# Moving transposes from TensorE to the DMA engines in a gated linear attention followed by a GELU layer, on one Trainium2 core

## The chip, the cores and the metric

The kernel runs on one core of one Trainium2 chip. The metric is the device time of one launch in microseconds (us), the median over runs. A profile of one execution gives what each engine did; its span runs from the first to the last instruction, and the execution's own time is a little longer than that span.

## The reference

```python
def _attn_ref(q, k, v, f_logit):                 # (4, 8, 768, 48) each
    f = 1.0 / (1.0 + np.exp(-f_logit))
    for t in range(S):
        state = f[:, :, t, :, None] * state + np.einsum('bhd,bhe->bhde', k[:, :, t], v[:, :, t])
        y[:, :, t] = np.einsum('bhd,bhde->bhe', q[:, :, t], state)
    return y

def _moe_ref(x, w_in, w_out):                    # (3072, 384), (384, 2048), (2048, 384)
    h = x @ w_in
    g = 0.5 * h * (1.0 + erf(h / sqrt(2)))
    return g @ w_out

def reference(**kwargs):
    attn_out = _attn_ref(q, k, v, f_logit)
    x = attn_out.transpose(0, 2, 1, 3).reshape(B * S, H * D)
    return _moe_ref(x, w_in, w_out)              # (3072, 384) float32
```

A recurrence over 768 steps with a decay per channel (4 batches, 8 heads, 48 channels) makes 3072 rows of 384 numbers. Each row then passes through a layer of 2048 hidden values with the exact GELU.

## The kernel before, in words

The 3072 rows are cut into 24 chunks of 128 rows; two chunks make a unit, so that there are 12 units, numbered from 0, and 6 chunks to a batch. Units 0, 1 and 2 are loaded in another layout ("pair"), with two neighbouring rows in one partition.

For each unit `decays` computes on ScalarE Exp (E) and Ln (L) of the logits; on TensorE the sums of the logs over the rows of a chunk (C, by products with triangular matrices); on ScalarE the exponentials of these sums, RG (to scale keys), GT (to scale queries) and GL (decay over a whole chunk); on VectorE the scaled keys KP and queries QP, in bf16; on GpSimd the cast of the values, VC.

`turn` transposes KP and QP. For each chunk TensorE makes four transposes of each (Tk, Tq: matmuls of 128x128 against an identity) into one PSUM bank, and VectorE copies the bank into the buffer `kq` (KQ). `attn_nat` (and `attn_pair` for pair units) then makes the scores (A, which reads `kq`), VectorE masks them (AM), TensorE updates the state (S; `carry` decays it on VectorE and GpSimd: R, T, SB) and multiplies scores and state with the values (Y, or YI and YX in pair units). `outputs` casts Y to bf16 on VectorE (YB), transposes it on TensorE (XT, three 128x128 matmuls) and copies it to the buffer `xT` on VectorE (X).

`ffn_group` takes the two chunks of a unit as a group of 256 rows. F1 is 8 operations of 6 matmuls of 128x256, each followed by one GELU on ScalarE (GE). F2 is, for each chunk, 4 operations of 4 matmuls of 128x384; the result leaves PSUM on ScalarE (O) and is stored (st). Exp and Ln share one ScalarE table and GELU needs another, so that each change between them costs a table load.

The order of the work on each engine is not written by hand. A planner (class `Plan`) knows for every operation an engine, an assumed duration, what it reads and writes, its buffers and a priority. It places operations greedily, those that can start first ahead of others, then by priority; what it makes is a fixed order of instructions on every engine. Engines then run this order and wait for each other through semaphores. The attention's operations have priority over those of the layer behind it. The planner treats DMAs as one more engine: `load` lists the loads in a fixed order (`LOADS`: units 0 and 1, the four blocks of `w_in`, unit 2, the four blocks of `w_out`, units 3 to 11), loads of inputs and stores of results are issued by SyncE's queue (SP), weights by GpSimd, and weights and inputs take turns by waiting for one another.

PSUM has 8 banks: four for F1 and F2 (`s_fh`), two for scores (`s_ap`), two for all else (`s_m`). There are 4 buffers for each of keys, queries and values, 3 for logits, 3 for `kq` and 4 for `xT`.

Of the kernel before, what the change touches and what calls it, by code (L numbers as in the profile page):

```python
# [16 lines left out]
TABLE = 1.28  # L17
# [40 lines left out]
class Op:  # L58
    __slots__ = ("eng", "dur", "fn", "bufs", "prio", "deps", "table", "start", "end", "vis", "seq", "name",
                 "left", "outs", "inst", "chain")  # L60


class Plan:
# [6 lines left out]
    def add(self, eng, dur, fn, rd=(), wr=(), bufs=(), prio=0.0, deps=(), table=None, name="", chain=None):  # L70
        o = Op()
        o.eng, o.dur, o.fn, o.bufs, o.prio, o.table, o.name = eng, dur, fn, tuple(bufs), prio, table, name
        o.start = o.end = o.vis = o.inst = None
        o.chain = chain
        o.seq = len(self.ops)
        d = list(deps) + ([chain] if chain else [])
        for k in rd:
            d += self.w.get(k, [])
        for k in wr:
            d += self.w.get(k, []) + self.r.get(k, [])  # L80
        for k in rd:
            self.r.setdefault(k, []).append(o)
        for k in wr:
            self.w[k] = [o]
            self.r[k] = []
        o.deps = list({id(x): x for x in d if x is not o}.values())
        for b in o.bufs:
            b.users.append(o)
        self.ops.append(o)
        return o  # L90

    def run(self):
        free = dict.fromkeys(list(LAT), 0.7)
        free["DMA"] = 1.8
        act = None
        for o in self.ops:
            o.outs = []
        for o in self.ops:
            o.left = len(o.deps)
            for d in o.deps:  # L100
                d.outs.append(o)
        ready = [o for o in self.ops if not o.left]
        placed = []
        while ready:
            best = None
            for o in ready:
                t = free[o.eng]
                for d in o.deps:
                    v = d.end if d.eng == o.eng and (o.eng != "DMA" or d is o.chain) else d.vis
                    t = v if v > t else t  # L110
                ok, taken = True, {}
                for b in o.bufs:
                    if b.slot is None:
                        v, k = b.slots.free(), taken.get(id(b.slots), 0)
                        if len(v) <= k:
                            ok = False
                            break
                        t = max(t, v[k][0])
                        taken[id(b.slots)] = k + 1
                if not ok:  # L120
                    continue
                x = t
                if o.table and act and o.table != act:
                    x = max(t, min(t + 2 * TABLE, max([d.vis for d in o.deps] + [0.0]) + PATIENCE))
                key = (int(x * 20 + 0.999), o.prio, o.seq)
                if best is None or key < best[0]:
                    best = (key, t, o)
            if best is None:
                raise RuntimeError("no operation can be placed: %s" % [o.name for o in ready[:20]])
            _, t, o = best  # L130
            d = o.dur
            if o.table and o.table != act:
                act = o.table
                d += TABLE
            o.start, o.end = t, t + d
            o.vis = o.end + LAT[o.eng]
            free[o.eng] = o.end
            for b in o.bufs:
                if b.slot is None:
                    b.slot = b.slots.free()[0][1]  # L140
                    b.slots.who[b.slot] = b
            ready.remove(o)
            placed.append(o)
            for n in o.outs:
                n.left -= 1
                if not n.left:
                    ready.append(n)
        if len(placed) != len(self.ops):
            raise RuntimeError("operations that wait for each other")
        placed.sort(key=lambda o: (o.start, o.seq))  # L150
        self.placed = placed
        return placed
# [4 lines left out]

SIZES = [2] * 12
PAIRS = [0, 1, 2]
LOADS = ["u0", "u1", "i0", "i1", "i2", "i3", "u2", "o0", "o1", "o2", "o3"]  # L160
# [4 lines left out]
def kernel(  # L165
# [172 lines left out]
    for what in LOADS:  # L338
        m = int(what[1:])
        if what[0] == "u":  # L340
            x = U[m]
            names = (("fl", f_logit), ("kt", k), ("qt", q), ("vt", v))
            if x["pair"]:
                for nm, a in names:
                    load("sp", lambda x=x, nm=nm, a=a, m=m: nc.sync.dma_start(  # L345
                        out=x[nm].t().rearrange("p (h x) -> p h x", h=H), in_=srcp(a, m)),
                        [(nm, 2 * m), (nm, 2 * m + 1)], [x[nm]], 1.2, f"{nm}{m}")
            else:
                for j in range(2):
                    for nm, a in names:  # L350
                        load("sp", lambda x=x, nm=nm, a=a, m=m, j=j: nc.sync.dma_start(
                            out=half(m, x[nm], j), in_=src(a, 2 * m + j)),
                            [(nm, 2 * m + j)], [x[nm]], 1.05, f"{nm}{m}.{j}")
        elif what[0] == "i":
            load("pool", lambda m=m: nc.gpsimd.dma_start(out=win[m], in_=win_src[:, :, 512 * m:512 * m + 512]),
                 [f"win{m}"], [], 2.2, what)
        else:
            load("pool", lambda m=m: nc.gpsimd.dma_start(out=wout[m], in_=wo_src[m]), [f"wout{m}"], [], 2.2, what)


    def decays(u):
# [6 lines left out]
        P.add("ACT", 0.72, lambda: nc.scalar.activation(fl.t(), fl.t(), AF.Exp, scale=-1.0),  # L368
# [5 lines left out]
        P.add("ACT", 0.72, lnop, rd=[("e", u)] + z_lf, wr=[("lf", u)], bufs=[fl, lf], table="exp", prio=pr, name=f"L{u}")  # L374
        gps = [s_m.new(), s_m.new()]
        for j, n in enumerate(ns):
# [5 lines left out]
            def cum(j=j, g=gps[j]):  # L382
# [9 lines left out]
                if j:  # L392
# [6 lines left out]
                  bufs=[lf, gps[j], gt, rg, y["kp"], y["qp"], gl], prio=pr, name=f"C{n}")  # L399
# [19 lines left out]
            P.add("POOL", 0.47, lambda y=y, j=j: nc.gpsimd.tensor_copy(  # L419
# [3 lines left out]
    St = {}  # L423

    def turn(u, kq):


        for j in range(2):
            n = 2 * u + j
            kp, qp = X[n]["kp"], X[n]["qp"]  # L430
            tp = s_m.new()
# [10 lines left out]
            def trans(i, sr, tpv=tpv):  # L442
                for p in range(P2):
                    nc.tensor.transpose(tpv()[:, i, p, :], sr.t()[:, 2 * p:2 * p + 2, :], ident)  # L444
            P.add("PE", 0.225, lambda kp=kp, trans=trans: trans(0, kp), rd=[("kp", n), "ident"], wr=[("tk", n)],
                  bufs=[tp, kp, kq], prio=pr + 4, name=f"Tk{n}")
            P.add("PE", 0.225, lambda qp=qp, trans=trans: trans(1, qp), rd=[("qp", n), "ident"], wr=[("tq", n)],
                  bufs=[tp, qp], prio=pr + 4, name=f"Tq{n}")
            P.add("DVE", 0.61, lambda tpv=tpv, kqv=kqv: nc.vector.tensor_copy(  # L449
# [11 lines left out]
    def carry(n, sp, mm, mmdur, mmrd, mmbufs, first_c):  # L461
# [4 lines left out]
        if mm is not None:  # L466
            P.add("PE", mmdur, mm, rd=mmrd, wr=[("sp", n)], bufs=[sp, tn] + mmbufs + ([] if first_c else [rr]),
                  prio=pr + 3.5, name=f"S{n}")
# [24 lines left out]
    def outputs(n, yp, pair):  # L493
# [3 lines left out]
        yb, xp = X[n]["yb"], s_m.new()  # L497
        P.add("DVE", 0.475, lambda: nc.vector.tensor_copy(yb.t(), yp.t()[:, 0:HD]),  # L498
              rd=[("yp", n)], wr=[("yb", n)], bufs=[yp, yb], prio=pr + 2, name=f"YB{n}")

# [6 lines left out]
        P.add("PE", 0.17, xmm, rd=[("yb", n), "ident"], wr=[("xp", n)], bufs=[yb, xp, xT], prio=pr + 1, name=f"XT{n}")  # L507

        def xcopy():
            to = xT.t()[:, :, j * C:(j + 1) * C]  # L510
            if pair:
                nc.vector.tensor_copy(to.rearrange("a i (p s) -> a i s p", s=2), xpv().rearrange("a i (s p) -> a i s p", s=2))
            else:
                nc.vector.tensor_copy(to, xpv())
        P.add("DVE", 0.27, xcopy, rd=[("xp", n)], wr=[("x", n)], bufs=[xp, xT], prio=pr + 1, name=f"X{n}")
# [6 lines left out]
    def attn_nat(u):  # L522
        kq = s_kq.new()
        turn(u, kq)
        for j in range(2):
# [11 lines left out]
            P.add("PE", 0.42, amm, rd=[("kq", n)], wr=[("ap", n)], bufs=[kq] + aps + ams, prio=pr + 3, name=f"A{n}")  # L537
# [13 lines left out]
            def ymm(j=j, ams=ams, vb=vb, yp=yp, osb=osb):  # L551
                if osb is not None:
                    inter(yp, lambda p: kq.t()[:, 1, p, j, :], osb, True)
                for hh in range(2):
# [5 lines left out]
            P.add("PE", 0.36 + (0.175 if c else 0), ymm,  # L560
                  rd=[("am", n, 0), ("am", n, 1), ("vb", n), ("kq", n)] + ([("sb", n - 1, 0), ("sb", n - 1, 1)] if c else []),
                  wr=[("yp", n)], bufs=[yp, x["yb"], vb, kq] + ams + ([osb] if c else []), prio=pr + 2, name=f"Y{n}")
            outputs(n, yp, False)

    def attn_pair(u):
# [8 lines left out]
        for jk in range(2):  # L574
            aps = [s_ap.new(), s_ap.new()]
            ams.append([s_am.new(), s_am.new()])

            def amm(jk=jk, aps=aps):
                for p in range(P2):
# [7 lines left out]
                  prio=pr + 3, name=f"A{u}.{jk}")  # L587
# [3 lines left out]
        def smm():  # L591
            for p in range(P2):
# [7 lines left out]
              wr=[("sp", n) for n in ns[:len(sps)]], bufs=sps + kps + vbs, prio=pr + 3.5, name=f"S{u}")  # L600
# [9 lines left out]
        def intra():  # L610
            for hh in range(2):
# [11 lines left out]
              prio=pr + 2, name=f"YI{u}")  # L623
        for cc, n in enumerate(ns):
# [3 lines left out]
            P.add("PE", 0.26, lambda cc=cc, o=o: inter(yps[cc], lambda p: kq.t()[:, 1, p, cc, :], o, False),  # L628
                  rd=[("yi", n), ("sb", n - 1, 0), ("sb", n - 1, 1)] + [("kq", m) for m in ns], wr=[("yp", n)],
                  bufs=[yps[cc], kq, o], prio=pr + 2 + 10 * cc, name=f"YX{n}")  # L630
        for cc, n in enumerate(ns):
            outputs(n, yps[cc], True)

    def ffn_group(g, gate):
# [10 lines left out]
        for u in range(FO // pk):  # L645
            hps = s_fh.new()

            def f1(u=u, hps=hps):
                for i in range(pk):
# [6 lines left out]
                  wr=[("h", g, u)], bufs=[xT, hps, gT], prio=pr, name=f"F1.{g}.{u}")  # L656
# [4 lines left out]
        for s_ in range(s):  # L661
# [11 lines left out]
            P.add("DMA", 0.55, lambda n=n, osb=osb: nc.sync.dma_start(out=out[n * C:(n + 1) * C, :], in_=osb.t()),  # L673
# [13 lines left out]
    state = {}  # L687
    for o in P.placed:
        if o.table and state.get("t") != o.table:
# [36 lines left out]
```

## Time and profile before

| | us |
|---|---|
| median of 3 runs (lowest to highest) | 203.27 (203.03 to 203.34) |
| the profiled execution's own time | 202.79 |
| its span | 200.9 |

| engine | busy us | share of the span | instructions |
|---|---|---|---|
| TensorE, matmuls (PE) | 182.2 | 91% | 2010 |
| TensorE, weight loads (PEld) | 141.7 | 71% | 2010 |
| VectorE (DVE) | 103.7 | 52% | 210 |
| ScalarE (ACT) | 143.4 | 71% | 243 |
| GpSimd (POOL) | 52.4 | 26% | 116 |

The time is 1.89 us above the span in the profiled execution, which itself is 0.48 us under the median. A line number such as L444 is a line of the kernel. "Landing" of a DMA is the time from its issue until its completion is seen. In a chain of waits each step is followed back to what released it; a share in it is a share of the way to the end, not of an engine's work. Shares of busy time are means over stages that differ: at the start the loads are awaited, in the middle the attention and the layer run together, and at the end only the layer is left.

### The profile page before, as it was taken

Reading aid. Unit: us, or ns where it says so; the run is one execution under the profiler, and the core shown is the slowest. Engines: PE = TensorE matmul, PEld = TensorE weight load, DVE = VectorE, ACT = ScalarE, POOL = GpSimd, SP = SyncE. Lnnn points to the kernel's source line nnn. Section 1 sums busy time; section 2 is a strip of 40 time slices with the busy share of each in tenths; the row PEclk is TensorE's granted clock in tenths of the full one; section 3 lists DMA queues with packets and bytes.
Section 4 is the critical chain, followed back from the end, with each engine's and each line's share of the span. In section 5 each row is a group of like instructions: output and inputs, shape, how many; then the busy total and the mean of one; then the engine's idle time right before and its main releaser. Section 6 shows DMA issues by size and latency. Waiting matters only on the chain.

```text
span 200.9 us, 4982 instructions
## 1 busy us (share of the span) xinstructions
PE 182.2 (91%) x2010; PEld 141.7 (71%) x2010; DVE 103.7 (52%) x210; ACT 143.4 (71%) x243; POOL 52.4 (26%) x116
## 2 busy tenths in 40 slices
PE   0677989999989997997999999999999999999992
PEld 0446667687678687666868958967877969696961
DVE  4479661274386685887559728759778400000000
ACT  3642069989899979986999999769565828273740
POOL 7369236041133434105145411115303000000000
PEclk9999999999999999999999999999999999999999
DMA  6999999999899989989999993011001011110102
GB/s 155 261 224 172 175 269 189 182 220 202 181 216 195 182 203 186 203 177 210 182 197 214 191 214 96 3 39 39 3 0 65 16 42 39 38 44 11 68 0 78
DMA packets 93013, 27.04 MB, mean 135 GB/s; under 512 B 87872, under 2 KB 92480, under 8 KB 92992
## 3 DMA queue, kind: packets, MB, share of 16 engines
q1 hardware_dynamic: 90816, 23.60, 53.7%
q0 software_dynamic: 2176, 3.15, 9.4%
q8 instruction: 15, 0.25, 0.5%
q14 instruction: 6, 0.05, 0.1%
HBM read 25.17 MB, written 4.72 MB: 149 GB/s over the span
## 4 chain that ended last, share of the span: by engine, by line
PE 57%; ACT 20%; DMA 13%; SPq 3%; issue 3%; DVE 2%; POOL 1%; ACTq 0%; DVEq 0%
PE ps L667 25%; PE ps L652 20%; ACT L692 8%; ACT gT L657 6%; DMA fl<-in_f_logit_dram 5%; DMA win<-in_moe_w_in_dram 4%; DMA kt<-in_k_dram 3%; PE ps L444 3%; SPq L345 2%; ACT fl L368 2%; PE ps L535 2%; ACT lf L373 2%; PE ps L506 1%; ACT rg L400 1%; PE ps L385 1%
## 5 line engine op out<-in xcount | busy, mean ns | idle before, releaser
L652 PE MATMUL ps<-xT,win 128*128 128x256 bf16 x576 | 72.7, 277 | 3.1 <-ACT gT L657 3.0
L667 PE MATMUL ps<-wout,gT 128*128 128x384 bf16 x384 | 70.1, 326 | 0.4 <-DMA wout<-in_moe_w_out_dram 0.2
L652 PEld LDWEIGHTS <-win 128*128 128x128 bf16 x576 | 61.4, 115 | 6.0 <-issue 3.5
L657 ACT ACTIVATE gT<-ps 128x512 bf16<-128x512 f32 x96 | 53.1, 602 | 7.9 <-PE ps L652 5.6
L667 PEld LDWEIGHTS <-gT 128*128 128x128 bf16 x384 | 35.1, 97 | 21.3 <-ACT gT L657 1.3
L692 ACT ACT_TABLE_LOAD x29 | 37.2, 1283 | 0.5
L413 DVE TENSOR_TENSOR kp<-kt,rg 128x384 bf16<-128x384 f32 x24 | 13.9, 579 | 24.1 <-ACT rg L400 24.0
L671 ACT ACTIVATE osb<-ps 128x384 f32<-128x384 f32 x24 | 11.8, 493 | 20.2 <-PE ps L667 20.0
L456 DVE TENSOR_TENSOR am<-ps,mask 128x512 bf16<-128x512 f32 x36 | 23.1, 684 | 5.9 <-PE ps L535 5.8
L419 POOL CAST vb<-vt 128x384 bf16<-128x384 f32 x24 | 13.1, 554 | 43.7 <-DMA vt<-in_v_dram 43.4
L482 POOL TENSOR_TENSOR tn<-rr,gl 128x384 f32<-128x384 f32 x16 | 13.6, 850 | 41.5 <-DVE rr L480 38.7
L368 ACT ACTIVATE fl<-fl 128x768 f32<-128x768 f32 x12 | 10.3, 859 | 18.0 <-DMA fl<-in_f_logit_dram 17.9
L498 DVE CAST yb<-ps 128x384 bf16<-128x384 f32 x24 | 13.0, 553 | 11.9 <-PE ps L557 9.0
L449 DVE COPY kq<-ps 128x1024 bf16<-128x1024 bf16 x24 | 16.4, 685 | 3.3 <-PE ps L444 3.1
L487 POOL CAST sb<-tn 48x192 bf16<-48x192 f32 x40 | 15.3, 383 | 8.4 <-DVE tn L476 6.5
L400 ACT ACTIVATE rg<-ps 128x384 f32<-128x384 f32 x24 | 11.9, 495 | 6.8 <-PE ps L387 3.5
L416 DVE TENSOR_TENSOR qp<-qt,gt 128x384 bf16<-128x384 f32 x24 | 14.4, 601 | 0.2 <-ACT gt L402 0.2
L402 ACT ACTIVATE gt<-ps 128x384 f32<-128x384 f32 x24 | 11.9, 496 | 0.0
L444 PE MATMUL ps<-ident,kp 128*128 128x128 bf16 x96 | 10.2, 234 | 0.3 <-DVE kp L413 0.3
L456 DVE TENSOR_TENSOR am<-ps,maskp 128x512 bf16<-128x512 f32 x12 | 7.7, 685 | 5.4 <-PE ps L583 5.4
L444 PE MATMUL ps<-ident,qp 128*128 128x128 bf16 x96 | 10.2, 234 | 0.3 <-DVE qp L416 0.3
L373 ACT ACTIVATE lf<-fl 128x768 bf16<-128x768 f32 x12 | 10.1, 843 | 0.3
(58 smaller groups left out, 150.6 us busy)
## 6 DMA issues: line engine op xcount, KB each, us to landing
out_dram<-osb SPq DMA_DIRECT2D x24, 192.0 KB, 1.9
fl<-in_f_logit_dram SPq DMA_DIRECT2D x18, 192.0 KB, 3.8
kt<-in_k_dram SPq DMA_DIRECT2D x18, 192.0 KB, 3.7
qt<-in_q_dram SPq DMA_DIRECT2D x18, 192.0 KB, 3.8
vt<-in_v_dram SPq DMA_DIRECT2D x18, 192.0 KB, 3.7
win<-in_moe_w_in_dram POOLq DMA_DIRECT2D x4, 384.0 KB, 8.2
wout<-in_moe_w_out_dram POOLq DMA_DIRECT2D x4, 384.0 KB, 6.7
fl<-in_f_logit_dram SPq DMA_DIRECT2D x3, 384.0 KB, 4.2
```

What stands on the lines that cost most here:

```text
L368: P.add("ACT", 0.72, lambda: nc.scalar.activation(fl.t(), fl.t(), AF.Exp, scale=-1.0), rd=[("fl", n) for n in ns], wr=[("e", u)], bufs=[fl ...
L373: nc.scalar.activation(lf.t()[:, :, :, 0:D], v, AF.Ln, bias=1.0)
L400: P.add("ACT", 0.40, lambda g=gps[j], rg=rg: nc.scalar.activation(rg.t(), g.t()[:, 0:HD], AF.Exp, scale=-1.0), rd=[("g", n)], wr=[("rg", n ...
L416: P.add("DVE", 0.475, lambda y=y, gt=gt, j=j: nc.vector.tensor_tensor(y["qp"].t()[:, :, 0:D], half(u, x["qt"], j), gt.t().rearrange("p (h ...
L444: nc.tensor.transpose(tpv()[:, i, p, :], sr.t()[:, 2 * p:2 * p + 2, :], ident)
L449: P.add("DVE", 0.61, lambda tpv=tpv, kqv=kqv: nc.vector.tensor_copy(kqv(), tpv().rearrange("a i p (c t) -> a (i p) c t", c=2) if U[u]["pai ...
L456: P.add("DVE", 0.61, lambda hh=hh: nc.vector.tensor_tensor(ams[hh].t(), aps[hh].t().rearrange("p (h t) -> p h t", t=C), mk.unsqueeze(1).to ...
L487: P.add("POOL", 0.36, lambda hh=hh: nc.gpsimd.tensor_copy(sb.t()[64 * hh:64 * hh + D, :, D * hh:D * hh + D], tn.t()[64 * hh:64 * hh + D, : ...
L652: nc.tensor.matmul(hps.t()[:, i * tok:(i + 1) * tok], col(fo)[:, kk, :], xT.t()[:, kk, :], start=(kk == 0), stop=(kk == KO - 1))
L657: acts.append(P.add("ACT", 0.50, lambda u=u, hps=hps: nc.scalar.activation(gT.t()[:, u * pk:(u + 1) * pk, :].rearrange("p a b -> p (a b)") ...
L667: nc.tensor.matmul(op.t()[:, 0:d_model], gT.t()[:, fo, s_ * C:(s_ + 1) * C], wout[fo // 4][:, fo % 4, :], start=(fo == 0), stop=(fo == FO ...
L692: nc.scalar.preload_act_table_set({"exp": "natural_log_exp_and_others", "gelu": "gelu_and_others"}[o.table])
```

## The change

- The outputs of units 3 to 11 are transposed by a DMA from SBUF to SBUF (`dma_start_transpose`, issued by SP) straight from `yb` to `xT`: 18 DMAs of 128x384 bf16 in place of 54 transposes on TensorE and 18 copies on VectorE.
- The keys and queries of units 6 to 11 are transposed in the same way from KP and QP to `kq`: 24 DMAs of 128x512 bf16 in place of 96 transposes on TensorE and 12 copies on VectorE.
- In units 0 and 1 ScalarE takes over the cast of the values from GpSimd and one chunk's KQ, YB and X copies from VectorE; in unit 0 the second pair of score banks, and in units 0 and 1 the banks of the sums, come from `s_fh`.
- In the gaps that the planner sees on TensorE in its first 30 us, matmuls of a zero tile are issued into the bank that the next operation opens; nobody reads them. There are 99.
- Results of pair units are stored with a row order that undoes the pair layout, so that X there is a plain copy.
- Many of the planner's assumed durations are changed, and the rule by which it delays a change of ScalarE's table; with the new operations this gives another order on every engine. ScalarE has 34 table loads in place of 30.

```diff
+EARLY = [0, 1]
+HELP = [0, 1]
+XDMA = [3, 4, 5, 6, 7, 8, 9, 10, 11]
+KDMA = [6, 7, 8, 9, 10, 11]
+WARM = 30.0
...
-                    v = d.end if d.eng == o.eng and (o.eng != "DMA" or d is o.chain) else d.vis
+                    v = d.end if d.eng == o.eng and (o.eng != "DMA" or d is o.chain) else d.vis + o.lag
...
-                    x = max(t, min(t + 2 * TABLE, max([d.vis for d in o.deps] + [0.0]) + PATIENCE))
+                    x = max(t, min(t + 2 * TABLE, max([d.vis for d in o.deps] + [switched]) + PATIENCE))
...
-        P.add("ACT", 0.72, lambda: nc.scalar.activation(fl.t(), fl.t(), AF.Exp, scale=-1.0),
+        P.add("ACT", 0.84, lambda: nc.scalar.activation(fl.t(), fl.t(), AF.Exp, scale=-1.0),
...
-        gps = [s_m.new(), s_m.new()]
+        gps = [(s_fh if u in EARLY else s_m).new() for _ in range(2)]
...
+            if u in KDMA:
+                for i, (key, sr) in enumerate((("kp", kp), ("qp", qp))):
+                    P.add("DMA", 0.6, lambda i=i, sr=sr, j=j: nc.sync.dma_start_transpose(
+                        kq.t()[:, i, :, j, :], sr.t().rearrange("p h d -> p (h d)")),
+                        rd=[(key, n)], wr=[("tk" if i else "kq", n)], bufs=[sr, kq], prio=-6, lag=1.3, name=f"{key}D{n}")
+                kqdeps[n] = [("tk", n), ("kq", n)]
+                continue
...
+        help_ = n // 2 in HELP and n % 2 == 1
+        P.add("ACT" if help_ else "DVE", 0.40 if help_ else 0.475, lambda: copier(help_)(yb.t(), yp.t()[:, 0:HD]),
...
+        if n // 2 in XDMA:
+            P.add("DMA", 0.5, lambda: nc.sync.dma_start_transpose(xT.t()[:, :, j * C:(j + 1) * C], yb.t()),
+                  rd=[("yb", n)], wr=[("x", n)], bufs=[yb, xT], prio=-7, lag=1.3, name=f"XD{n}")
+            return
...
-            aps = [s_ap.new(), s_ap.new()]
+            aps = [(s_fh if jk and u == 0 else s_ap).new() for _ in range(2)]
...
-            P.add("DMA", 0.55, lambda n=n, osb=osb: nc.sync.dma_start(out=out[n * C:(n + 1) * C, :], in_=osb.t()),
+            P.add("DMA", 0.55, lambda n=n, osb=osb: nc.sync.dma_start(out=rows(n), in_=osb.t()),
...
+    junk = one.tile([C, C], BF16, name="junk")
+    nc.gpsimd.memset(junk, 0.0)
+    at = 0.9
     for o in P.placed:
+        if o.eng == "PE":
+            if o.opens is not None and o.start < WARM:
+                for _ in range(int((o.start - at - 0.25) / (0.11 if o.start < 10 else 0.06))):
+                    nc.tensor.matmul(o.opens.t()[:, 0:C], junk, junk, start=True, stop=True, skip_group_check=True)
+            at = o.end
```

## The prediction

> **What bounds it now.** I read the table of stretches first, since a mean hides stages. Columns: length; busy us (instructions) of PE, PEld, DVE, ACT, POOL; granted clock; DMA share; GB/s.
>
> ```profile
> 0.00:37.00 37.00, 26.33 (x319) 19.21 (x320) 20.47 (x54) 18.09 (x29) 19.86 (x53) 1.00 1.08 207
> 37.00:120.00 83.00, 78.99 (x934) 61.37 (x933) 53.36 (x100) 76.71 (x126) 24.41 (x48) 1.00 0.95 197
> 120.00:160.00 40.00, 39.62 (x484) 32.34 (x483) 29.92 (x56) 29.14 (x56) 8.12 (x15) 1.00 0.11 36
> 160.00:200.90 40.90, 37.29 (x280) 28.76 (x277) 0.00 (x0) 19.45 (x34) 0.00 (x0) 1.00 0.11 39
> ```
>
> From 37 to 120 us three things are nearly full: PE 95%, ACT 92%, DMA 95%. From 120 us on PE alone is full. So less work on PE helps at once in the last 80 us, but in the middle it meets ACT and DMA at once. The chain of waits shows the closing part, pure layer work without a gap, with the last product's start:
>
> ```profile
> 160.77 5.20 PE ps L667 x32
> 165.97 5.24 PE ps L652 x48
> 171.21 5.20 PE ps L667 x32
> ...
> 192.09 5.21 PE ps L667 x32
> 197.37 0.49 ACT osb L671
> ```
>
> The tail after 197.4 (one copy, one store) is 3.5 us and stays. The timeline of the start, ScalarE and TensorE:
>
> ```profile
> 22.56 2.75 PE L652 MATMUL ps<-xT,win 128*128 128x256 bf16 x12
> 25.81 1.93 PE L652 MATMUL ps<-xT,win 128*128 128x256 bf16 x12
> 27.02 0.85 ACT L368 ACTIVATE fl<-fl 128x768 f32<-128x768 f32 x1 [10.53 <-DMA fl<-in_f_logit_dram]
> 29.18 3.04 ACT L657 ACTIVATE gT<-ps 128x512 bf16<-128x512 f32 x6
> 33.60 0.82 PE L667 MATMUL ps<-wout,gT 128*128 128x384 bf16 x4 [0.17 <-DMA wout<-in_moe_w_out_dram]
> ```
>
> The same 12 matmuls take 2.75 us, then 1.93; later in the chain they take 1.31. ACT stands 10.5 us before unit 2's Exp, with the first GELUs queued behind it. The first F2 waits for `w_out`, at 33.6. The loads before that do not change.
>
> **PE's sum.** The chain's prices are start to start: the eight transposes of a chunk's keys and queries (L444) take 0.45, the three of its outputs (L506) 0.17.
>
> ```profile
> 40.41 0.45 PE ps L444 x8
> ...
> 50.27 0.17 PE ps L506 x3
> ```
>
> Removed: 12 chunks x 0.45 = 5.4 and 18 x 0.17 = 3.1, together 8.5 us. The order of the changed program has 78 F1 matmuls and unit 2's sums ahead of the first F2, against 54 and no sums before: 24 x 0.109 + 0.9 = 3.5 us of work done while PE waits for `w_out`. That is possible because ACT now runs all 8 GELUs of group 0 before unit 2's Exp, in the 10.5 us hole. If the hole did not hold them, this 3.5 goes. PE alone would then end at 197.4 - 8.5 - 3.5 = 185.4, with the same losses as before.
>
> The 99 unread matmuls cost 99 x 0.056 = 5.5 us warm (1.31/12 halves for 128 columns), 10 us at the slow rate of 2.75/12; all stand ahead of the first F2, in PE's idle time (10.7 us of 37). Bounds: a gain of about 2 us, as early matmuls run at 1.31 and not at 2.75, to a loss of 2 where a gap is shorter than planned. I take zero: both end before the wait for `w_out`. The copies moved to ACT (10 of some 0.5 us) also lie in its hole; the banks taken from `s_fh` likewise, as F1 starts later. The pair units' plain X copies (351 ns instead of 588) save 6 x 0.24 us on VectorE, which is 52% busy: nothing.
>
> **ACT's sum.** This is what I expect to be late next. From unit 2's Exp to the start of unit 11's Exp the old order holds 24 table loads, 48 GELUs, 9 E, 9 L, 30 RG/GT, 14 GL, 12 O. Start to start in the timeline these take 1.28, 0.52, 0.86, 0.84, 0.385, 0.19, 0.42: 90.2 us, in 95.1 us of time (27.0 to 122.1), so 5% is lost. The new order holds 28 table loads, 56 GELUs, 36 RG/GT, 17 GL, 16 O: 104.1 us, with the same loss 109.7, so unit 11's Exp starts at 136.7. To the last GL another 10.8: 147.5. The last sums on PE end 1.2 earlier, at 146.3. Behind them the new order has 168 F1 matmuls x 0.109, 128 F2 x 0.1625 and 2.3 us of attention: 41.4. PE ends at 187.7, 2.3 later than by its own sum.
>
> **DMA's sum.** The queue of SP issues 72 loads and 10 stores from 37.3 to 118.8: 0.99 us each, at 95% DMA share. Unit 11's last logits are issued at 115.2 and land 2.9 later. The new order puts 28 transposes (16 of 128 KB, 12 of 96 KB) and 4 more stores ahead of that load. The trace holds no transposing DMA. Lower bound: a store's 0.36 us on SP. Upper bound: 1.9 us, a store's time to landing, if none overlaps the next. By bytes, beside a load (192 KB in 0.99 us), 128 KB is 0.67 and 96 KB 0.50: 0.60 on average. I take 0.6 because the loads are the nearest row in size and share the queue. Then that load lands at 115.2 + 1.4 + 28 x 0.6 + 2.9 = 136.3: just ahead of ACT's 136.7, so no slack is left, and each further 0.1 us per transpose adds 2.8 us to the end.
>
> Here the pages speak. The Trainium skill, "VectorE: DVE Perf Modes", section "The three transpose paths", gives 1309 ns for one 128x128 bf16 block by DMA against 390 ns on TensorE, and its rules prefer TensorE where PSUM will do; paid block after block, the 100 blocks ahead of that load would be 131 us and the kernel would end near 300. "DMA: Bandwidth & Descriptors", section "Latency and other measured facts", gives 261 GB/s for transposing DMAs, by which the two kinds would be an estimated 0.50 and 0.38 us, and DMA would not bind. The trace decides between neither.
>
> **New waits.** Scores wait for a DMA instead of a copy. The chain is RG 0.5, KP 0.58, QP 0.6, then landing (loads 3.8 median, 5.5 at most; stores 1.9). Between a unit's sums and its scores the new order holds 7 us of PE work or more, except 3.6 in unit 7 and 4.1 in unit 8. With 3.8 the chain is 5.5: short by 1.9 and 1.4. F1 of groups 3 to 6 has 3.8, 5.3, 4.8, 4.5 us behind the last Y; cast and landing take 4.5: 0.7 short once. Of these 4 us most fall while PE waits for ACT anyway; I add 1. On SP each transpose waits for VectorE, and the loads behind it wait too; that is in the 0.99 only for stores (SP waited 13.1 us in sum to issue those). Range for it: 0 to 8 us.
>
> **Sum.** 187.7 + 1 + 3.5 = 192.2 span; 1.9 more gives 194.1 beside the profiled 202.79; the median lay 0.5 over that. Forecast 194.
>
> **Rivals.**
> 1. PE alone sets the end, because ACT's waits shrink when sums arrive earlier: 185.4 + 3.5 + 1.9 = 190.8. For it: ACT stood 3.2 us for logits in the middle. Against: four more table loads. Chance 0.17.
> 2. Slower: DMA becomes the bound. From 0.93 us per transpose the gain of 9 is gone (9/28 above 0.6). At 1.9 the load lands at 172.7, the end is 36 later: 230. For it: a 95% share already; against: by bytes it is too small. Chance 0.26, from 204 to 230.
> 3. Landing near 5.5 us: chains of 7.2, scores short by 3.6, 3.1 and 0.2, F1 (6.2 with the cast) by 2.4, 0.9, 1.4, 1.7: 13.3 in place of the 1 that I added, 206 if nothing hides it, 200 if half lies beside ACT's waits. Chance 0.12; half of it is faster, a quarter no change.
>
> The forecast itself has 0.45, 191 to 199.
>
> **Numbers.** 0.2% is about what a measurement of this kernel can tell from no change. Faster: 0.45 + 0.17 + 0.06 = 0.68; same 0.03; slower 0.26 + 0.03 = 0.29. The range reaches from 188 (rival 1 with the unread matmuls' gain) to 212, which is 1.2 us per transpose; about 0.05 lies below and 0.13 above.
>
> **What would show it.** Right: first GELU near 20 us, unit 2's Exp still at 27, first F2 at 33 to 34; transposes landing in 2 to 4 us; unit 11's Exp near 137; PE gapless for its last 41 us. Wrong: DMA share full past 140 us and ACT or PE waiting for logits (rival 2); PE or weight loads waiting for `kq` or `xT` over 8 us in sum (rival 3); an Exp of unit 11 before 132 (rival 1). A first F2 past 35 us voids the early 3.5.

## The result, and the profile after

| | us | ratio to before (95% interval) |
|---|---|---|
| before, median of 4 runs (lowest to highest) | 203.31 (203.03 to 204.09) | |
| the changed kernel, median of 4 runs | 229.89 (226.68 to 231.41) | 1.119 (1.109 to 1.129) |
| its profiled execution: own time, span | 231.12, 229.4 | |

The change makes the kernel 12% slower. The forecast was 194.0 with a range of 188 to 212, so the time lies outside the range on the slow side. (The medians are over all executions, the ratios here and below over the undisturbed ones alone: 226.68 and 228.67 for the changed kernel, whose profiled execution is a slower one, and in what follows 5 of e3's 10, 8 of e11's 10 and 3 of e12's 4.)

The table of stretches of the changed kernel answers to the first view of the prediction. The columns are again length; busy us (instructions) of PE, PEld, DVE, ACT, POOL; granted clock; DMA share; GB/s.

```profile
0.00:37.00 37.00, 30.64 (x440) 25.51 (x441) 16.37 (x48) 26.53 (x44) 17.61 (x50) 0.95 1.06 205
37.00:120.00 83.00, 69.18 (x698) 49.97 (x695) 36.77 (x65) 55.89 (x91) 16.64 (x33) 0.90 0.70 147
120.00:160.00 40.00, 29.41 (x310) 22.65 (x310) 18.36 (x32) 32.67 (x54) 7.61 (x13) 0.96 0.81 156
160.00:188.50 28.50, 22.82 (x206) 16.60 (x202) 10.22 (x17) 20.05 (x32) 7.08 (x14) 0.88 0.58 123
188.50:229.40 40.90, 36.53 (x315) 28.51 (x312) 6.68 (x12) 20.76 (x39) 1.51 (x3) 1.00 0.21 60
```

In the mean over 37 to 120 us nothing is full any more: PE 83%, ACT 67%, DMA 0.70, where they stood at 95%, 92% and 0.95. In those 83 us PE executes 698 matmuls in place of 934. No engine is the bound of the whole stretch; all of them wait. The clock fell too, from 1.00 to 0.90 and 0.88. From 120 to 188 us DMA is still at work (0.81 and 0.58, before 0.11; from 140 to 160 us it is 0.96), so the loads are late, and the attention ends far later.

The chain that ended last shows for what PE waits in the middle, and that the closing part is what it was:

```profile
100.61 2.58 PE ps L681 x12
...
111.45 2.45 DMA kq<-qp
...
135.05 4.56 DMA kq<-qp
...
153.10 3.83 DMA fl<-in_f_logit_dram
...
204.96 5.24 PE ps L681 x48
210.20 5.20 PE ps L696 x32
```

The last group's blocks take 5.24 and 5.20 us as before, so the loss lies wholly ahead of them. In the middle the chain goes through the landing of transposed keys and queries and of logits. The first line shows a second price of waiting: 12 F1 matmuls, 1.31 us at full clock, took 2.58 when PE had stood still for 3.1 us before them; the granted clock from 100.6 to 103.2 us is 0.55.

The queue of SP tells where the lateness begins (start, duration, line, operation):

```profile
43.52 1.32 SPq L702 DMA_DIRECT2D out_dram<-osb  x2
44.90 2.27 SPq L358 DMA_DIRECT2D vt<-in_v_dram  x1
47.22 3.84 SPq L358 DMA_DIRECT2D fl<-in_f_logit_dram  x1
51.10 2.89 SPq L358 DMA_DIRECT2D kt<-in_k_dram  x1
...
110.13 1.22 SPq L451 DMA_TRANSPOSE kq<-kp  x1
111.45 1.22 SPq L451 DMA_TRANSPOSE kq<-qp  x1
112.77 1.21 SPq L529 DMA_TRANSPOSE xT<-yb  x1
114.02 0.57 SPq L358 DMA_DIRECT2D qt<-in_q_dram  x1
```

Two separate things are to be seen. Right behind the first two stores of pair units, loads that elsewhere take 0.5 to 0.7 us hold the queue for 2.3 to 3.8 us each; no transposing DMA has run yet, the first starts at 73.3. And later each transposing DMA holds the queue for 1.2 us, twice what a load takes. Unit 11's last logits are issued at 167.74, in the kernel before at 115.17. The stretch table for the time right behind those stores:

```profile
44.50:46.00 1.50, 1.50 (x15) 0.78 (x12) 0.80 (x2) 0.60 (x1) 0.00 (x0) 1.00 0.12 25
46.00:47.20 1.20, 1.20 (x23) 0.79 (x23) 0.76 (x2) 0.00 (x0) 0.00 (x0) 1.00 0.12 31
```

DMA share 0.12 at 25 to 31 GB/s, while loads stand in the queue. In the kernel before, right behind its first two stores (44.1 to 46.0), it was 0.83 at 236 GB/s. 0.12 of 16 engines is two engines. The new store of pair units writes `out` through a view `j p m` of 2 x 64 x 384, whose outermost dimension is 2.

### The profile page after: what moved, and what is told of

It reads as the page before. It is cut to its first block, busy times and chain, and to the rows that moved or that the text cites. A ratio compares the mean times of both kernels' runs of the same rounds, so it can differ in the third digit from the quotient of the medians.

```text
span 229.4 us, 4917 instructions
## 1 busy us (share of the span) xinstructions
PE 188.6 (82%) x1959; PEld 143.2 (62%) x1959; DVE 88.4 (39%) x174; ACT 155.9 (68%) x257; POOL 50.4 (22%) x113
## 4 chain that ended last, share of the span: by engine, by line
PE 38%; DMA 14%; DVE 1%; issue 1%; SPq 1%; ACT 1%; ACTq 0%; DVEq 0%
PE ps L681 18%; PE ps L696 15%; DMA kq<-qp 11%; PE ps L564 2%; DMA fl<-in_f_logit_dram 2%; DMA xT<-yb 1%; PE ps L586 1%; PE ps L548 1%; SPq L529 1%; PE ps L574 1%; PE ps L392 0%; DVE am L482 0%; ACT fl L375 0%; SPq L451 0%; DVE rr L506 0%
## 5 line engine op out<-in xcount | busy, mean ns | idle before, releaser
L681 PE MATMUL ps<-xT,win 128*128 128x256 bf16 x576 | 81.1, 299 | 7.3 <-DMA xT<-yb 6.3
L681 PEld LDWEIGHTS <-win 128*128 128x128 bf16 x576 | 64.2, 120 | 15.5 <-DMA xT<-yb 5.6
L686 ACT ACTIVATE gT<-ps 128x512 bf16<-128x512 f32 x96 | 55.1, 598 | 24.3 <-PE ps L681 22.4
L696 PEld LDWEIGHTS <-gT 128*128 128x128 bf16 x384 | 36.5, 100 | 22.1 <-issue 1.7
L427 POOL CAST vb<-vt 128x384 bf16<-128x384 f32 x20 | 10.6, 535 | 97.4 <-DMA vt<-in_v_dram 97.4
L508 POOL TENSOR_TENSOR tn<-rr,gl 128x384 f32<-128x384 f32 x16 | 13.7, 859 | 35.4 <-DVE rr L506 32.1
L375 ACT ACTIVATE fl<-fl 128x768 f32<-128x768 f32 x12 | 10.2, 850 | 15.3 <-DMA fl<-in_f_logit_dram 15.2
L564 PE MATMUL ps<-kq 64*128 64x128 bf16 x144 | 7.4, 222 | 16.0 <-DMA kq<-qp 16.0
L564 PEld LDWEIGHTS <-kq 64*128 64x128 bf16 x144 | 4.9, 95 | 19.3 <-issue 10.9
L392 PE MATMUL ps<-lf,trin 128*128 128x384 bf16 x18 | 6.1, 360 | 7.9 <-ACT lf L380 7.7
L506 DVE TENSOR_TENSOR rr<-ps,tn 128x384 f32<-128x384 f32 x16 | 8.9, 553 | 5.8 <-PE ps L574 4.4
L394 PEld LDWEIGHTS <-lf 128*128 128x128 bf16 x72 | 4.3, 101 | 9.9 <-issue 8.8
```

What stands on the lines that cost most here:

```text
L508: P.add("POOL", 0.83, lambda: nc.gpsimd.tensor_tensor(tn.t(), rr.t(), glb(), ALU.mult), rd=[("rr", n), ("gl", n)], wr=[("tn", n)], bufs=[r ...
L564: nc.tensor.matmul(aps[hh].t()[:, p * C:(p + 1) * C], kq.t()[r, 0, p, j, :], kq.t()[r, 1, p, j, :], start=True, stop=True)
L681: nc.tensor.matmul(hps.t()[:, i * tok:(i + 1) * tok], col(fo)[:, kk, :], xT.t()[:, kk, :], start=(kk == 0), stop=(kk == KO - 1))
L686: acts.append(P.add("ACT", 0.50, lambda u=u, hps=hps: nc.scalar.activation(gT.t()[:, u * pk:(u + 1) * pk, :].rearrange("p a b -> p (a b)") ...
L696: nc.tensor.matmul(op.t()[:, 0:d_model], gT.t()[:, fo, s_ * C:(s_ + 1) * C], wout[fo // 4][:, fo % 4, :], start=(fo == 0), stop=(fo == FO ...
```

## The experiments

Three theories were put against each other. The store (S): the row-ordering store of the units 0 to 2, which rides along in the diff, delays the loads behind it. The queue (Q): each transposing DMA holds SP longer than the 0.6 us assumed, so loads come late and everything behind them. The landing (L): loads are not the matter, PE waits for the transposed data themselves. Runs are compared with the kernel before in the same session (202.8 to 204.0 us).

**Both parts undone, one by one.** In `e1_store_split` the new store is cut into two DMAs of 64 partitions; bytes and row order stay, the outermost dimension of each is 64.

```diff
+    def store(n, o):
+        r = out[n * C:(n + 1) * C, :]
+        if not U[n // 2]["pair"]:
+            return nc.sync.dma_start(out=r, in_=o)
+        for j in range(2):
+            nc.sync.dma_start(out=r.rearrange("(p j) m -> j p m", j=2)[j], in_=o[64 * j:64 * j + 64])
...
-            ... nc.sync.dma_start(out=rows(n), in_=osb.t()),
+            ... store(n, osb.t()),
```

> The changed kernel, but each result of a pair unit is stored by two DMAs of 64 partitions in place of one whose outermost dimension is 2. Theory S (the new store runs on few DMA engines and holds the loads queued behind it: after the two stores at 43.5 us the DMA share falls to 0.09): unit 6's first logits, issued at 86.6 us, are issued at 68 to 75; the time falls from 228 by 8 to 18, to 210 to 220. Theory Q (the 42 transposes hold SP's queue 1.2 us each, and this is the whole loss): the time stays above 224. Theory L (waits of scores and F1 for the landing): the same, above 224.

`e2_no_transposes` keeps the new store and takes the transposing DMAs out; `e3_split_no_transposes` does both.

```diff
-XDMA = [3, 4, 5, 6, 7, 8, 9, 10, 11]
-KDMA = [6, 7, 8, 9, 10, 11]
+XDMA = []
+KDMA = []
```

> The changed kernel without any DMA transpose (both lists empty), the new store kept. Theory S: the loads are still late by some 20 us at unit 6, the time is 206 to 216. Theory Q or L alone: all of the loss is gone, 194 to 199.

> No DMA transposes, and the split store: what is left is the early part (copies on ScalarE, unread matmuls, banks, other durations). All theories: 194 to 201, by the early lead of some 3 us and ScalarE's additional table loads. If it is above 204, the early part or the new order of the work costs by itself.

`e4_before_new_store` is the kernel before with nothing but the new store (and the plain X copy that goes with it).

```diff
+    def rows(n):
+        r = out[n * C:(n + 1) * C, :]
+        return r.rearrange("(p j) m -> j p m", j=2) if U[n // 2]["pair"] else r
...
-            ... nc.sync.dma_start(out=out[n * C:(n + 1) * C, :], in_=osb.t()),
+            ... nc.sync.dma_start(out=rows(n), in_=osb.t()),
```

> The kernel before, with only the new store of pair units (and the plain X copy that goes with it). Theory S: 208 to 220, with load issues of 2 to 4 us on SP behind each pair store and unit 6's first logits issued at 75 us or later in place of 64.8. Theories Q and L: 203, no change.

| kernel | median us (lowest to highest) | ratio (95%) | last logits issued |
|---|---|---|---|
| the changed kernel | 229.89 (226.68 to 231.41) | 1.119 (1.109 to 1.129) | 167.74 |
| e1, store split | 214.43 (212.48 to 215.13) | 1.051 (1.043 to 1.060) | 151.76 |
| e2, no transposing DMA | 217.91 (217.20 to 218.37) | 1.070 (1.063 to 1.076) | 134.42 |
| e3, both | 202.98 (199.93 to 206.13) | 0.986 (0.981 to 0.991) | 118.71 |
| e4, before with the new store | 218.95 (218.61 to 219.08) | 1.075 (1.068 to 1.081) | 131.15 |

By the medians the four corners add up. The store costs 229.9 - 214.4 = 15.5 us with the transposing DMAs, 217.9 - 203.0 = 14.9 without them, and 219.0 - 203.1 = 15.8 in the kernel before. The transposing DMAs cost 214.4 - 203.0 = 11.4 with the split store and 229.9 - 217.9 = 12.0 with the other. By the ratios, each 0.01 being 2.03 us, they add up less well: the store costs 13.8, 17.1 and 15.3, the transposing DMAs 13.2 and 10.0, each some 3 us less beside the other. So there are two causes, the store the larger one, and they overlap little.

How six stores of 192 KB each can cost 15 us is seen in SP's queue in e4:

```profile
42.82 1.30 SPq L674 DMA_DIRECT2D out_dram<-osb  x2
44.18 2.15 SPq L351 DMA_DIRECT2D kt<-in_k_dram  x1
46.38 4.46 SPq L351 DMA_DIRECT2D qt<-in_q_dram  x1
50.88 3.01 SPq L351 DMA_DIRECT2D vt<-in_v_dram  x1
```

Three loads take 9.6 us where three undelayed ones take 2.1 (0.7 each). Behind the next stores the queue shows a load of 2.12, a store of 3.23 (others 0.34) and a load of 4.35: 9.7 in place of 1.8. Behind those of unit 2 two loads take 3.07 and 3.87: 6.9 in place of 1.4. Together the queue is held 7.5 + 7.9 + 5.5 = 20.9 us longer; the last logits come 16.0 us later and the end 15.8. The rest met time in which SP stood waiting for other engines anyway: from 37 us to the last logits such waits are 39.6 us in the kernel before and 29.7 in e4. The stretch behind the first stores, first in e4, then in e1 with the split store:

```profile
44.20:45.50 1.30, 1.30 (x15) 1.30 (x13) 1.02 (x2) 0.74 (x2) 0.26 (x1) 1.00 0.12 26
```

```profile
44.50:46.00 1.50, 1.50 (x20) 0.79 (x20) 0.68 (x2) 0.60 (x1) 0.00 (x0) 1.00 0.60 144
```

Same bytes, same rows in `out`: what differs is the outermost dimension, 2 against 64 (and that there are two DMAs in place of one), and the share is 0.12 against 0.60. The Trainium skill, "DMA: Bandwidth & Descriptors", section "Why a DMA increments its semaphore by 16 and not by 1", says that the number of engines a DMA runs on is the largest number up to 16 that divides the outermost dimension on both sides; its "Rules for kernel authors" warn of an outermost dimension below 16. For this store it gives two engines, 2/16 = 0.125, and the traces agree. Why the queue also stops taking the loads behind it is not shown by it; the queue's rows show that it does.

**Which transposes cost.** `e5_outputs_only` is e1 with `KDMA = []` (18 DMAs of outputs), `e6_keys_queries_only` e1 with `XDMA = []` (24 of keys and queries). `e7_priced` is e1 with the planner told 1.3 us on the queue for each instead of 0.5 and 0.6, and a lag of 0.6 instead of 1.3, so that it orders the work by the measured price.

> Split store, DMA transposes of the outputs alone (18 DMAs, none for keys and queries). Without any transposes this kernel took 203.0 us, with both kinds 214.4. Theory Q (each transpose holds SP's queue for 1.2 us, and loads and stores come late): 12 of the 18 stand ahead of the last logits, 15 us of queue, of which part meets slack: 205 to 210. Theory L (the waits for landing are the loss, and those of F1 for xT were 12 us in the changed kernel against 23 for kq): 203 to 207.

> Split store, DMA transposes of keys and queries alone (24 DMAs). Theory Q: 16 ahead of the last logits, 20 us of queue: 206 to 211. Theory L: scores wait for kq some 25 us in sum as in the run with both: 210 to 216. If this and the run with outputs alone each cost little (under 3 us), but both together 11, the queue has a threshold, which speaks for Q.

> Split store and all 42 transposes, but the planner is told 1.3 us of queue for each (0.6 and 0.5 before), with the same time until they are seen (2.9 us). Theory Q with a wrong plan (the order was made for a queue that is twice as fast): 204 to 210. Theory Q with the queue as a hard limit, or L: 211 to 216, as with the old prices.

| kernel | median us (lowest to highest) | ratio (95%) | last logits issued |
|---|---|---|---|
| e5, outputs only | 201.17 (200.10 to 201.51) | 0.987 (0.981 to 0.993) | 127.71 |
| e6, keys and queries only | 208.57 (206.61 to 209.48) | 1.023 (1.014 to 1.031) | 135.31 |
| e7, e1 priced | 213.91 (213.20 to 214.28) | 1.050 (1.043 to 1.057) | 166.52 |

The outputs' DMAs cost nothing: e5 lies at e3's ratio, 9 us of later logits notwithstanding, and it beats both kernels. It is the version to keep, though by the ratios it is no better than e3, which has no transposing DMA at all. Keys and queries cost 208.6 - 203.0 = 5.6 (7.5 by the ratios); both together 11.4 (13.2), more than the sum of the parts. A likely reading, not tested by itself, is that e5's lateness still fits into slack and that what comes on top of it does not. A planner that knows the price changes nothing (213.9 against 214.4): it moves the last logits even further back.

**The queue by itself.** `e8_unread_transposes` is e3 with 28 transposing DMAs of 128 KB on SP, behind the loads of keys and values of units 5 to 11, into scratch tiles that nobody reads; `e9_unread_one_block` the same with one block of 128x128 each, a quarter of the bytes. No instruction waits for their data, and TensorE's work is e3's.

```diff
+                u = int(name[2:].split(".")[0])
+                if u >= 5 and name[:2] in ("kt", "vt"):
...
+                    nc.sync.dma_start_transpose(d, win[0][:, 0, :])                  # e8
+                    nc.sync.dma_start_transpose(d[:, 0, :], win[0][:, 0, 0:C])      # e9
```

> Split store, all real transposes on TensorE as without the change, and 28 DMA transposes of 128x512 bf16 that nobody reads and that wait for no engine's data, one behind every second load of units 5 to 11 on SP. TensorE's work and waits are as in the run of 203.0. Theory Q: 28 x 1.2 us = 34 us more queue, the last logits issued at 140 to 152 in place of 118.7, time 208 to 218. Theory L: 202 to 205.

> As the run with 28 unread transposes (228.3 us, last logits issued at 144.8), but each moves one 128x128 block (32 KB) in place of four. If SP's time per instruction is the price (1.2 us for three blocks and for four alike): 1.2 us again, last logits at 135 to 145, 220 to 229. If the price goes with the bytes: 0.3 to 0.5 us on SP, last logits under 128, 203 to 210.

| kernel | median us (lowest to highest) | ratio (95%) | last logits issued |
|---|---|---|---|
| e8, 28 unread, 128 KB | 228.32 (227.49 to 229.97) | 1.122 (1.114 to 1.130) | 144.77 |
| e9, 28 unread, 32 KB | 222.70 (221.16 to 224.06) | 1.098 (1.092 to 1.104) | 139.65 |

Transposes for which nobody waits cost 25.3 and 19.7 us over e3 (27.7 and 22.8 by the ratios). So lateness on the queue alone is enough; no landing is needed. The last logits move 26.1 and 20.9 us, about as much as the end. The expectation for e8 was too low. SP in e9:

```profile
98.64 0.53 SPq L367 DMA_DIRECT2D kt<-in_k_dram  x1
99.20 1.30 SPq L340 DMA_TRANSPOSE dummy<-win  x1
100.60 0.53 SPq L367 DMA_DIRECT2D qt<-in_q_dram  x1
```

One block takes 1.30 us (median of the 28: 1.34, least 1.22), where in the changed kernel three blocks have a median of 1.21 and four blocks 1.21 and 1.28. In e8, where the DMA engines are full, four blocks have a median of 1.50 and a least of 1.30. So the price is nearly all one of the instruction: four times the bytes add 0.16 us. SP goes from one to the next with hardly a gap, so the queue is the limit, while the engines behind it have room in e9. The same stretch in e8 and in e9:

```profile
100.00:120.00 20.00, 19.24 (x207) 15.04 (x208) 13.28 (x26) 15.37 (x28) 4.19 (x9) 0.83 0.96 187
```

```profile
100.00:120.00 20.00, 18.45 (x214) 14.42 (x212) 14.08 (x27) 14.62 (x25) 5.14 (x11) 0.95 0.78 163
```

With 128 KB each the DMA engines are full (0.96), with 32 KB they are not (0.78). Most of the cost, 19.7 of 25.3 us, stays when three quarters of the bytes go.

**The landing.** `e11_late_keys` is e1 with `KDMA = [9, 10, 11]`: six chunks' keys and queries, late enough that the loads are as late as in e5. `e12_keys_queries_together` is e1 with keys and queries of a chunk in one tile and one DMA of 8 blocks, so 30 transposing DMAs in place of 42.

```diff
+                both = X[n]["both"]
+                P.add("DMA", 0.6, lambda both=both, j=j: nc.sync.dma_start_transpose(
+                    kq.t().rearrange("a i p c t -> a (i p) c t")[:, :, j, :], both.t().rearrange("p i h d -> p (i h d)")),
```

> Split store, DMA transposes of the outputs from unit 3 on, of keys and queries from unit 9 on only, which stand on SP where nearly all loads are gone. With outputs alone it took 201.2 us. Theory Q: TensorE saves 6 x 0.45 = 2.7 us and no load is held: 198 to 201. Theory L (the landing of kq costs by itself): 202 to 206.

> Split store, all outputs, keys and queries transposed by DMA as in the run of 214.4 us, but a chunk's keys and queries lie in one tile and go as one DMA of 128x1024, so that there are 30 DMAs in place of 42. If the price is per instruction: 12 x 1.25 = 15 us less queue, some 10 of it ahead of the last logits, 206 to 211. If it goes with the bytes: 212 to 216.

| kernel | median us (lowest to highest) | ratio (95%) | last logits issued |
|---|---|---|---|
| e11, keys and queries from unit 9 | 204.80 (202.76 to 208.67) | 1.007 (1.004 to 1.010) | 127.76 |
| e12, one DMA for both | 209.77 (207.43 to 210.62) | 1.031 (1.025 to 1.037) | 150.72 |

e11 and e5 issue the last logits at the same time, 127.8 and 127.7, and e11 has 48 transposes fewer on PE, yet it takes 3.6 us more (4.1 by the ratios). Its waits (what waited, for what: us in all, times, longest):

```profile
PE ps L564 <- DMA kq<-qp: 7.4, 4, 3.0
PEld L564 <- DMA kq<-kp: 4.0, 2, 3.2
```

So waiting for landings costs something too, most likely some us beyond what TensorE saves (the planner's order of the work differs as well). In e12 twelve DMAs fewer bring 4.7 us over e1, 0.39 for each; one DMA of 8 blocks holds SP for a median of 1.27 us, again like one block, but lands after 3.5 us (2.8 and 2.4 for the two halves in the changed kernel), and PE waits 11.8 us for it in sum, the weight loads 13.2. The gain is well below 12 x 1.2 = 14.4.

**What sets the end.** That unread transposes delay the end through the queue does not tell what sets the end in e1. Here are pieces of the chain that ended last, first in e8, where L340 is the unread transposes, then in e1:

```profile
138.29 1.85 SPq L340
...
144.77 2.97 DMA fl<-in_f_logit_dram
147.76 0.84 ACT fl L384
```

```profile
146.73 2.44 DMA kq<-qp
...
156.07 2.45 DMA kq<-qp
...
163.07 2.45 DMA kq<-qp
...
175.27 2.44 DMA kq<-qp
```

In e8 the chain runs along SP's queue to the last logits and on to their Exp. In e1 the last logits, issued at 151.76, are not in the chain: it passes one landing of transposed queries after another, with TensorE's work between them, and these landings make up 9.6% of its span, 20 us (in the changed kernel 11.0%, 25 us). Nor does the end follow the last logits where the transposes are read: against e3 they come 33 us later in e1 and 48 in e7, while the kernels are 11.4 and 10.9 us slower. SP is not only held by its DMAs either: in e1, from 37 us to the last logits, it stands 20 us for other engines ahead of transposes and 3.3 ahead of loads, while in e3 it stands 26.7 us ahead of loads. So it is shown that a held queue is enough to make the kernel late, and that waiting for landings costs something; how the loss of the transposing DMAs in e1 divides between the two is not shown.

**The unread matmuls.** `e10_no_unread_matmuls` is e3 with `WARM = 0.0`.

> Split store, no DMA transposes, and none of the 99 unread matmuls. With them it took 203.0 us. If they warm TensorE to some use, the first F1 starts later and the time is 204 to 206; if they are in the way (unit 2's Exp started at 31.0 us with them, 27.0 before the change), 200 to 202; if neither, 203.

202.44 us (201.08 to 203.44), ratio 0.997 (0.994 to 1.001), against 202.98 for e3, whose runs reach from 199.93 to 206.13. By the medians the unread matmuls make it 0.5 us slower, by the ratios (0.986 for e3) 1.1% faster: no effect that these runs can tell. The median of e3 is hardly below the kernel before (203.1 in that session), so its ratio of 0.986 is not firm either; which of the rest of the early part (copies on ScalarE, banks, plain X copies) would bring it was not tried alone.

## Why the prediction was wrong

**The step that failed outright: the stores.** The prediction lists "the pair units' plain X copies ... nothing" and never prices the store that makes the copy plain. That store costs 14 to 17 us, more than half of the loss of 26.6. It was a part of the diff, its outermost dimension of 2 could be read there, and the DMA share of 0.95 showed that the queue had little room for a slower store.

**The term that was mis-sized: 0.6 us for each transpose.** It was taken "because the loads are the nearest row in size": an argument by bytes, for something that does not go by bytes. Measured: 1.2 to 1.5 us of SP for each instruction in the median, with one block or eight. The text had said where that decides: from 0.93 on the gain is gone, 1.2 gives 212. By its own sum, 1.2 gives 194.1 + 28 x 0.6 = 210.9; e1, which has the transposes without the store, ran at 214.4. The last logits would be issued at 115.2 + 1.4 + 28 x 1.2 = 150.2; e1 shows 151.76. Both come near, but that does not confirm the path of the sum: e1's chain does not pass through the last logits, and e7 issues them 14.8 us later than e1 and ends no later. The size of the term is shown; that the end follows the queue is shown for the unread transposes alone, and in e1 the nearness may be luck. What else makes e1's loss is not taken apart; its waits of PE for `kq` (16.0 us in all) and its clock of 0.952 are the candidates.

**The price by block and the price by bytes.** The Trainium skill's 1309 ns for a block by DMA ("VectorE: DVE Perf Modes", "The three transpose paths") lies close to the 1.34 us for which e9's single block holds the queue (it lands 3.1 us after its issue), but four or eight blocks hold it hardly longer, so paid block after block it was far too dear (near 300), and its 261 GB/s ("DMA: Bandwidth & Descriptors", "Latency and other measured facts") was too cheap: 128 KB in 1.2 us of the queue is 107 GB/s. The traces bear out neither: it is nearly all a price of the instruction.

**ScalarE's sum (the forecast's bound).** It was never reached: unit 11's Exp was to start at 136.7, but its logits are issued at 167.74 in the changed kernel and at 151.76 in e1. ACT waits 15.2 us for logits in the changed kernel, where it waited 7.4 before if the 10.5 ahead of unit 2 are left out.

**TensorE's sum.** The removed 8.5 us are gone (matmul instructions 2010 to 1959, with 99 unread ones added), but PE was not what the middle waited for. The early 3.5 us were void, by the sign given for it ("A first F2 past 35 us"):

```profile
35.44 1.46 PE L696 MATMUL ps<-wout,gT 128*128 128x384 bf16 x8
```

Unit 2's Exp starts at 31.1 instead of 27 (in e3, whose early part is the same, at 31.0): ScalarE's hole did not hold the GELUs of group 0. In e3 the first starts at 21.49 and not near 20, the eight end at 29.3 with gaps in which ScalarE waits for F1, and a copy of X and a table load stand behind them. F1 itself was slow at that time: in the changed kernel 12 of its matmuls took 2.73 us at 19.79, at a granted clock of 0.54.

**The new waits.** 1 us was added, with 0 to 8 as the range. The waits of the changed kernel:

```profile
PE ps L564 <- DMA kq<-qp: 16.0, 9, 4.7
PEld L564 <- DMA kq<-kp: 7.5, 5, 3.1
PE ps L681 <- DMA xT<-yb: 6.3, 3, 3.1
PEld L681 <- DMA xT<-yb: 5.6, 2, 3.3
```

That is 35.4 us in sum, far over the 8 us by which the prediction would tell its third rival. The landing itself was well placed, medians of 2.8 us for keys, 2.4 for queries and 3.1 for outputs, under the 3.8 that was reckoned with. What failed is that most of the waiting would fall beside ACT's: landings of queries stand in the last chain with 25 us. How much of this is a transpose issued late by the queue, and how much the landing by itself, is not separated; e11 gives 3.6 us for six chunks, with what TensorE saves already taken off.

**The rivals.** The second one happened in kind: loads came late, held up in SP's queue, and its sign ("DMA share full past 140 us") came, with 0.96 from 140 to 160 us and 0.71 from 160 to 180. Its price by transposes alone would have been 212; the 230 that it names as its end was reached through the store, of which it knew nothing. So the rival was right about the smaller half of the loss, and its far end was met by accident. The first rival (PE alone) did not come. The third came in its sign (35.4 us of waits) and not in its cause, a landing near 5.5 us; how large its part is stays open.

**What held:** the closing part is gapless, in blocks of 5.2 us, though for the last 31 us of PE and not 41; the unread matmuls are worth zero within what can be measured.

## What to carry to other kernels

Price every DMA that a diff touches, also those that only make another copy cheaper, and look at its outermost dimension: where the queue is full, a store that runs on two engines is paid by the loads behind it. When loads and other DMAs share one queue, count instructions and not bytes, and ask for each what stands behind it; a smaller number of such DMAs (e5's 18 of outputs) can be free where 42 are not. Where one price that no row shows decides the sign, its range and not its likeliest value should set the chances.

## What the runs showed of the hardware that was not expected

- A transposing DMA from SBUF to SBUF holds SP's queue for some 1.2 to 1.5 us whether it moves 1, 3, 4 or 8 blocks of 128x128 (medians 1.34, 1.21, 1.21 to 1.50, 1.27), where undelayed loads of 192 KB take 0.53 to 0.7. It lands 2.4 to 3.5 us after its issue.
- A store whose outermost dimension is 2 leaves the DMA share at 0.12 and holds the loads behind it for 2 to 4.5 us each; cut into two DMAs with outermost dimension 64 it does not, at 0.6 us of SP each.
- A stall of PE can cost a second time: 12 F1 matmuls right behind a wait of 3.1 us took 2.58 us instead of 1.31, at a granted clock of 0.55. The mean granted clock was 0.933 in the changed kernel, 0.952 in e1 and 0.988 in e3.
